# Attention with a top-32 mask, then a mixture of experts, on one core: another order for the scores, one VectorE shift, the reads of the value sums and the late tails of the transposes

## The chip, the cores and the metric

The kernel runs on one core of one Trainium2 chip. The metric is the device time of one execution in microseconds (us). The core has five engines with queues of their own: TensorE (PE, with its weight loads as PEld), VectorE (DVE), ScalarE (ACT), GpSimd (POOL) and SyncE (SP, which issues most transfers). Each engine takes its instructions strictly in the order in which they are written in the kernel; between engines only waits on semaphores keep order.

## The reference, cut to what matters

```python
# attention: q, k, v are (2, 8, 576, 64)
scores = scale * np.matmul(q, k.transpose(0, 1, 3, 2))
kth = np.partition(scores, -32, axis=-1)[..., -32:-31]
scores = np.where(scores >= kth, scores, -1e9)
scores = scores - np.max(scores, axis=-1, keepdims=True)
attn = np.exp(scores)
attn = attn / (np.sum(attn, axis=-1, keepdims=True) + 1e-09)
x = np.matmul(attn, v)          # then reshaped to (1152, 512)
# mixture of 8 experts: each token goes to the expert of its largest logit
h = np.maximum(np.einsum('ecd,edf->ecf', disp, w1), 0.0)
y = np.einsum('ecf,efd->ecd', h, w2)
out[i] = gate_w[i] * y[expert_idx[i], pos[i]]
```

## The kernel before, in words

Attention is worked off in 36 units. A unit `u` is one block of 128 query rows (9 blocks) with one pair of heads (4 pairs); heads of a pair are `j` = 0 and 1, each row has 576 scores. The function `attention` runs a loop of 35 iterations; unit 35 and the leftovers follow by hand. In iteration `i` different steps of different units stand beside each other (a software pipeline), and the order of the calls in this loop is the order in every engine's queue:

- `scores(u)`: PE multiplies queries and keys into three PSUM banks, tile `s0` (two banks: all of head 0, and the first 64 columns of head 1) and tile `s1` (the other 512 columns of head 1). There is one copy of these tiles, so `scores(i+1)`, issued in iteration `i`, has to wait until everything that reads unit `i`'s scores is through.
- `heads(i)`: DVE takes the 8 largest of each 64-column segment (18 MAX8, L312), then the row maximum `mx` (L315), a masked copy (L316), and at the end the shift "max minus score" of 64 columns of head 1 into the tile `sm` (L318). These 64 columns lie in the second bank of `s0`.
- `shift(i)`: ACT shifts the remaining columns, 576 of head 0 out of `s0` and 512 of head 1 out of `s1` (two activations, L353).
- `merge(i)`: DVE looks for the pivot among the segments' maxima (MAX8 `ns` L329, MATCH_REPLACE8 L334, MAX8 L336 and L337); `bound` finishes it one iteration later.
- `sign(i-1)` and `turn(i-1)`: ACT counts, POOL multiplies, giving the tile `z`; `select(i-2)`: DVE takes two MAX8 over 576 columns of `z` (steps 1 and 2, L393), and two small steps to the threshold `nk` (L397).
- `penalty(i-3)`: ACT writes the tile `pen` (two activations, L406) from `nk`; `probs(i-3)`: PE transposes `sm` plus `pen` in 9 blocks (L425, L426), ACT takes the exponential (L427).
- `values(i-4)`: PE multiplies with the values (L447, L450) into the bank `pV`, in two halves (one per head); `normalise(i-5)` on DVE reads it (L461, L463, L466).
- `route(t, stage)`: the router of a finished block of tokens, in stages over some eight iterations: stage 0 transposes on PE, stage 0.5 copies them with ACT (`copies()`, L519), stage 1 multiplies with the gate (L522), stages 2 to 2.2 pick the expert, 3 to 5.5 find the slot and scatter the row.

Short DVE steps (`small`: `bound`, `select` 0, `normalise`, router steps, the picks of experts in `early` and `late`) are taken one after another between the 18 MAX8 of `heads`: `fill()` issues the next one, 16 times per unit; what is left follows after `heads`.

Iterations 3 to 30 hold the 9 transposed blocks in one PSUM tile `p3` (`whole` is true). In iterations 31 to 34 they go in three steps of 4, 4 and 1 blocks; the last one, the tail, then uses columns 384 to 511 of the bank `pV` and is issued after `scores(i+1)`. From iteration 31 on PE also works on the first expert in quarters (`quarter_h`, L654; ACT takes the result at L701).

The order on PE in an iteration is: transposes of `probs(i-3)`, `values(i-4)`, router stages 1 and 3, `scores(i+1)`, (late tail), router stage 0. After attention the experts follow, bound to the routed tokens.

Of the kernel before, what the change touches and what calls it, by code (L numbers as in the profile page):

```python
# [19 lines left out]
FT = mybir.dt.float32  # L20
# [5 lines left out]
OP = mybir.AluOpType  # L26
BIG = float(2.0 ** 90)
LOW = -3.0e38
# [7 lines left out]
def kernel(  # L36
# [11 lines left out]
    nc = tc.nc  # L48
    B, H, S, D = q.shape
# [13 lines left out]
    P = {}  # L63
# [14 lines left out]
    def att(*a, **k):  # L78
        return P["att", 0].tile(*a, **k)
# [31 lines left out]
    TAIL = S - 512  # L111
# [173 lines left out]
    PS, VAL, SM, Z, NK, PEN, PT = {}, {}, {}, {}, {}, {}, {}  # L285
# [18 lines left out]
    def heads(u, fill):  # L304
        un = UN[u % 2]
        nn = att([128, 2, SEG, 5], FT, name="nn")
        SM[u] = att([128, 2, S], FT, name="sm", tag="sm", bufs=4)
        mx = att([128, 4, 2], FT, name="mx4", bufs=3)
        for j in range(2):
            for i in range(SEG):  # L310
                o = int(i < FOUR)
                nc.vector.max(out=un[:, j, i, o:o + 8], in_=segment(u, j, i))  # L312
                if i < SEG - 1:
                    fill()
        nc.vector.tensor_reduce(out=mx[:, 0], in_=un[:, :, :, 0:2], axis=mybir.AxisListType.XY, op=OP.max)  # L315
        nc.vector.scalar_tensor_tensor(nn, un[:, :, :, 0:5], -1.0, keep[:, None].to_broadcast([128, 2, SEG, 5]),  # L316
                                       op0=OP.mult, op1=OP.min)
        nc.vector.tensor_scalar(SM[u][:, 1, :TAIL], PS[u][0][:, S:S + TAIL], -1.0, mx[:, 0, 1:2], op0=OP.mult, op1=OP.add)  # L318
        VAL[u] = [mx, un, nn.rearrange("p j s c -> p j (s c)")]

    def merge(u, fill):
        mx, un, nn = VAL[u]
        wk = att([128, 2, 5 * SEG], FT, name="wk")
        na = att([128, 2, 8], FT, name="na")
        tm = att([128, 2, 8], FT, name="tm")
        ns = att([128, 2, 8], FT, name="ns")
        vb = VB[u % 2]
        for j in range(2):
            nc.vector.max(out=ns[:, j], in_=nn[:, j])  # L329
        if u == NU - 1:  # L330
            fill()
        fill()
        for j in range(2):
            nc.vector.match_replace(out=wk[:, j], in_to_replace=ns[:, j], in_values=nn[:, j], imm_value=LOW)  # L334
        for j in range(2):
            nc.vector.max(out=vb[:, j], in_=un[:, j, :, 5:])  # L336
            nc.vector.max(out=na[:, j], in_=wk[:, j])  # L337
        fill()
        VAL[u] = [mx, na, vb, tm]
# [11 lines left out]
    def shift(u):  # L351
        for j, (o, i) in enumerate(((SM[u][:, 0], PS[u][0][:, :S]), (SM[u][:, 1, TAIL:], PS[u][1]))):
            nc.scalar.activation(o, i, AF.Identity, bias=VAL[u][0][:, 0, j:j + 1], scale=-1.0)  # L353

    SEL, SG = {}, {}

# [53 lines left out]
    def probs(u, *steps):  # L410
        sm = SM[u].rearrange("p j s -> p (j s)")
        pen = PEN[u].rearrange("p j s -> p (j s)")
        whole = ("p3", 0) in P
        if 0 in steps:
            PT[u] = att([128, 9, 128], FT, name="pT", tag="pT")
        for step in (0,) if whole else steps:
            if whole:
                bs, pt = range(9), P["p3", 0].tile([128, 9, 128], FT, name="p3", bufs=1)
            elif step < 2:
                bs, pt = range(5 * step, 5 * step + 4), bank4()  # L420
            else:
                bs, pt = (4,), pv[:, None, 384:512]
            for i, c in enumerate(bs):
                cs = slice(128 * c, 128 * c + 128)
                nc.tensor.matmul(pt[:, i], sm[:, cs], ident, start=True, stop=False, is_transpose=True)  # L425
                nc.tensor.matmul(pt[:, i], pen[:, cs], identB, start=False, stop=True)  # L426
            nc.scalar.activation(PT[u][:, bs[0]:bs[-1] + 1], pt, AF.Exp, scale=-scale)  # L427

    PV, XR = {}, {}
    pv = psum.tile([128, 512], FT, name="pV", bufs=1)  # L430
# [42 lines left out]
    TAIL_P = []  # L473
# [448 lines left out]
    NU = NT * HP  # L922
# [120 lines left out]
    def attention(side, early, late, mid, act, pool, end):  # L1043
        nc.vector.memset(OHS, 0.0)
        def run(fs):
            for f, *a in fs:
                f(*a)

        for i in range(NU - 1):
            if i == FUSED[0]:  # L1050
                swap_psum("pt", "p3")
            if i == FUSED[1]:
                swap_psum("p3", "pt")
            whole = ("p3", 0) in P

            def routes(stages):
                res = []
                for st in stages:
                    t, r = divmod(i - 6 - int(st), HP)
                    if r == HP - 1 and 0 <= t < NT:  # L1060
                        res.append((route, t, st, nc.vector if t == NT - 1 else nc.gpsimd))
                return res

            def copies():
                t, r = divmod(i - 7, HP)
                return [(route, t, 0.5, None)] if r == HP - 1 and t >= 0 else []

            def at(lag, f, *a):
                return [(f, i - lag) + a] if 0 <= i - lag < NU else []

            small = []

            def fill():
                if small:
                    run([small.pop(0)])

            small += at(1, bound, 0) + at(1, bound, 1) + at(1, bound, 2) + at(2, select, 0) + early.get(i, [])
            small += at(5, normalise, 0) + at(5, normalise, 1) + at(5, normalise, 2) + routes((2, 2.1, 2.2, 4, 5, 5.5)) + late.get(i, [])
            run((copies() + at(3, penalty) if whole else at(3, penalty) + copies()) + at(0, heads, fill))
            while small:  # L1080
                fill()
            run((at(1, sign_turn, act.get(i, []), pool.get(i, [])) if i > 1 else []) + side.get(i, []))
            last = i == NU - 2
            exps, tails = (at(3, probs, 0), []) if whole else (at(3, probs, 0, 1), at(3, probs, 2))
            run(exps + at(0, shift) if last else at(0, shift) + exps)
            run(at(4, values) + routes((1, 1.5, 3)) + at(-1, scores) + tails + routes((0, 3.5)))
            run(mid.get(i, []) + at(2, select, 1) + at(2, select, 2))
            small += at(2, select, 3) + at(2, select, 4)
            if last:
                small += [(route, NT - 3, 2, nc.gpsimd)]  # L1090
            run(at(0, merge, fill))
            while small:
                fill()
            run(end.get(i, []))
            if last:
                values(i - 3)


        L, T = NU - 1, NT - 1
        small = []  # L1100
# [31 lines left out]
        drop()  # L1132
        run(side.get(L, []))
        shift(L)
        penalty(L - 2, (1,))
        merge(L, fill)
        swap_psum("sc", "bk")
# [98 lines left out]
    pt = [bank1().bitcast(HF) for _ in range(2)]  # L1236
# [149 lines left out]
```

## Time and profile before

| | us |
|---|---|
| median of 3 runs (lowest to highest) | 385.41 (385.14 to 385.71) |
| time of the profiled execution | 387.18 |
| its span, first to last instruction | 385.4 |
| busy in the span: PE / PEld | 327.9 / 266.8 |
| busy in the span: DVE / ACT / POOL | 320.5 / 277.9 / 240.0 |

The profiled execution is one of its own, so its time stands 1.8 us above the median; some 1.8 us of it lie around the span. Times of instructions below are us from the start of the span. In rows of the timeline the first number is the start, the second the duration, then engine, line, operation, the tiles as out<-in, their shape, and in brackets how long the engine sat idle before it and what ended that.

### The profile page before, as it was taken

The page shows a single profiled execution, that of the slowest core. Times are in us where ns is not written, and L with a number is a line of the kernel's source. Part 1 is how long each engine was busy: PE and PEld are TensorE (multiplying, and loading weights), DVE is VectorE, ACT ScalarE, POOL GpSimd, SP SyncE. Part 2 cuts the span into 40 slices and gives each one's busy share as a digit, 9 for nine tenths or more (in the row PEclk, how much of TensorE's full clock was granted, in tenths as well). Part 3 has the DMA queues.
Part 4 walks back from the last instruction along what each step waited for, and adds up shares of the span by engine and source line. Part 5 has one row for each costly group of instructions (what it writes and reads, how often), then busy time and mean ns, then how long its engine had stood idle before and what let it go on. Part 6 is the DMA issues. An engine that isn't in the chain of part 4 may idle for free. (4 is left out here: it accounts for less than half of the span.)

```text
span 385.4 us, 9927 instructions
## 1 busy us (share of the span) xinstructions
PE 327.9 (85%) x3383; PEld 266.8 (69%) x3383; DVE 320.5 (83%) x1708; ACT 277.9 (72%) x464; POOL 240.0 (62%) x280
## 2 busy tenths in 40 slices
PE   5676978797888887978898889898879999999991
PEld 3454857585766765756586678788834899997781
DVE  4888699999999999999999998857664778799940
ACT  5788688888887878888789587766256649586810
POOL 3975868588886697988988788964301101119521
PEclk9778699999999999999989899989999999999997
DMA  9629996937282920000211730730849999999400
GB/s 153 133 63 195 219 199 203 207 113 125 40 265 79 344 106 3 30 2 29 57 54 44 225 117 28 247 111 29 295 144 268 204 351 401 340 300 400 83 23 23
DMA packets 69922, 60.25 MB, mean 156 GB/s; under 512 B 52069, under 2 KB 52069, under 8 KB 69863
## 3 DMA queue, kind: packets, MB, share of 16 engines
q1 hardware_dynamic: 67719, 54.79, 52.0%
q0 software_dynamic: 1616, 4.73, 3.4%
q8 instruction: 28, 0.46, 0.5%
q14 instruction: 31, 0.25, 0.2%
q10 hardware_dynamic: 528, 0.02, 0.1%
HBM read 40.66 MB, written 12.09 MB: 137 GB/s over the span
## 5 line engine op out<-in xcount | busy, mean ns | idle before, releaser
L312 DVE MAX8 un<-s 128x8 f32<-128x64 f32 x648 | 107.1, 216 | 12.8 <-PE s L294 12.8
L369 POOL TENSOR_TENSOR z<-sm,sg 128x576 f32<-128x576 f32 x71 | 89.5, 1280 | 24.0 <-ACT sg L362 22.0
L674 POOL DMA_INDIRECT out_dram<-y,xp x12 | 25.5, 2122 | 79.3 <-DVE y L850 39.1
L450 PE MATMUL pV<-vm,pT 128*128 128x65 f32 (+1 forms) x640 | 69.9, 267 | 0.0
L450 PEld LDWEIGHTS pV<-vm,pT 128*128 128x128 f32 (+1 forms) x640 | 68.9, 186 | 0.0
L353 ACT ACTIVATE sm<-s,mx 128x576 f32<-128x576 f32 x72 | 47.4, 710 | 25.4 <-DVE sm L318 23.6
L615 DVE TENSOR_TENSOR ws<-wr,ws 128x1024 bf16<-128x1024 f32 x52 | 60.7, 1215 | 2.6 <-ACT ws L609 2.5
L425 PE MATMUL p<-ident,sm 128*128 128x128 f32 x252 | 52.3, 293 | 9.8 <-ACT pT L427 5.6
L362 ACT ACTIVATE sg<-sm,mx 128x576 bf16<-128x576 f32 x72 | 55.0, 766 | 3.1 <-DVE mx L348 2.6
L426 PE MATMUL p<-identB,pen 128*128 128x128 bf16 x252 | 47.2, 227 | 9.8 <-ACT pen L406 9.8
L294 PE MATMUL s<-qk 128*128 128x512 f16 (+3 forms) x320 | 45.7, 301 | 8.7 <-ACT sm L353 8.6
L406 ACT ACTIVATE pen<-sm,nk 128x576 bf16<-128x576 f32 x71 | 51.2, 769 | 2.4 <-DVE nk L397 0.9
L425 PEld LDWEIGHTS p<-ident,sm 128*128 128x128 f32 x252 | 37.0, 147 | 22.0 <-ACT pT L427 12.3
L609 ACT ACTIVATE ws<-wr 128x2048 f16<-128x2048 f32 (+1 forms) x26 | 47.6, 1842 | 5.3 <-issue 4.4
L393 DVE MAX8 z<-z 128x8 f32<-128x576 f32 x72 | 50.8, 745 | 0.0
L654 PEld LDWEIGHTS <-ws 128*128 128x128 f16 (+1 forms) x768 | 48.8, 98 | 1.0 <-issue 0.4
L426 PEld LDWEIGHTS <-pen 128*128 128x128 bf16 x324 | 34.3, 108 | 16.1 <-ACT pen L406 14.3
L294 PEld LDWEIGHTS <-qk 128*128 128x128 f16 (+1 forms) x320 | 20.5, 108 | 20.1 <-issue 12.4
L427 ACT ACTIVATE pT<-p 128x1152 f32<-128x1152 f32 x28 | 31.6, 1130 | 0.0
L615 POOL TENSOR_TENSOR ws<-wr,ws 128x1024 bf16<-128x1024 f32 x12 | 25.6, 2132 | 0.0
L447 PE MATMUL pV<-vt,pT 128*128 128x130 f32 (+1 forms) x80 | 18.4, 313 | 4.9 <-DVE pD L960 1.8
L835 PEld LDWEIGHTS <-ws 128*128 128x128 f16 (+1 forms) x288 | 21.3, 98 | 0.0
(273 smaller groups left out, 640.9 us busy)
## 6 DMA issues: line engine op xcount, KB each, us to landing
wr<-in_moe_w_dram SPq DMA_DIRECT2D x32, 1024.0 KB, 6.2
xbuf<-zero SPq DMA_DIRECT2D x6, 771.0 KB, 5.0
qnat<-in_q_dram SPq DMA_DIRECT2D x16, 144.0 KB, 3.8
knat<-in_k_dram SPq DMA_DIRECT2D x16, 144.0 KB, 4.1
out_dram<-zero SPq DMA_DIRECT2D x3, 768.0 KB, 4.7
vm<-in_v_dram SPq DMA_DIRECT2D x16, 128.0 KB, 3.0
qk<-qk SPq DMA_DIRECT2D x14, 144.0 KB, 2.4
vt<-in_v_dram SPq DMA_DIRECT2D x4, 64.0 KB, 3.1
```

The costliest lines, as they stand in the source:

```text
L294: nc.tensor.matmul(PS[u][a][row:row + n, o:o + w], QK[b][2 * i][:, h, s:s + n], QK[b][1][:, h, c:c + w], start=(i == 0), stop=(i == 1))
L312: nc.vector.max(out=un[:, j, i, o:o + 8], in_=segment(u, j, i))
L362: nc.scalar.activation(SG[u][j], SM[u][:, j], AF.Sign, bias=VAL[u][0][:, 2, j:j + 1], scale=-(1.0 - 2.0 ** -20), accum_out=CNT[:, c:c + 1])
L369: engs[j].tensor_tensor(out=Z[u][:, j], in0=SM[u][:, j], in1=SG[u][j], op=OP.mult)
L393: nc.vector.max(out=z8[:, step - 1], in_=Z[u][:, step - 1])
L406: eng.activation(o, x, AF.Relu, bias=n)
L425: nc.tensor.matmul(pt[:, i], sm[:, cs], ident, start=True, stop=False, is_transpose=True)
L426: nc.tensor.matmul(pt[:, i], pen[:, cs], identB, start=False, stop=True)
L450: nc.tensor.matmul(PV[t][row:row + n, h0 + half], PT[u][:, 5 * half + c, row:row + n], VM[b][:, c, p, half], start=False, stop=(half == 1 ...
L609: nc.scalar.activation(w[:, 0, s], r[:, s], AF.Copy)
L615: eng.tensor_tensor(out=w[:, 1].bitcast(BF)[:, s], in0=r[:, s], in1=w[:, 0, s], op=OP.subtract)
L654: nc.tensor.matmul(o, a(i), c(i), start=(i == 0 and m == 0), stop=(i == k - 1 and m == 2))
```

## The change

Four things are moved, nothing is computed differently:

1. `values(i-4)` is cut: half 0 stands before `scores(i+1)`, half 1 and all router stages behind it.
2. The 64-column shift leaves `heads` and becomes `shift_rest`. On DVE the order after `heads` is now: `select` step 1 (first MAX8 over `z`), the two `ns` maxima of `merge` (half 0), `shift_rest`, `select` step 2 (second MAX8 over `z`), then the rest of `merge` (half 1). In the order of the kernel the 64-column shift now stands behind ACT's `shift`.
3. In the list `small`, `early` and `late` come ahead of `normalise`, filled up with empty entries to at least four, so that `normalise` and the router's reads come four fills later.
4. The tail of the transposes gets a bank of its own (`ex`) in iterations 31 to 34 and is issued with the other two steps; in all iterations `penalty` stands ahead of `copies()` on ACT.

```diff
-        nc.vector.tensor_scalar(SM[u][:, 1, :TAIL], PS[u][0][:, S:S + TAIL], -1.0, mx[:, 0, 1:2], op0=OP.mult, op1=OP.add)
...
+    def shift_rest(u):
+        nc.vector.tensor_scalar(SM[u][:, 1, :TAIL], PS[u][0][:, S:S + TAIL], -1.0, VAL[u][0][:, 0, 1:2],
+                                op0=OP.mult, op1=OP.add)
...
-    def merge(u, fill):
-        mx, un, nn = VAL[u]
+    def merge(u, fill, half=None):
+        mx, un, nn = VAL[u][:3]
+        if half != 1:
+            ns = att([128, 2, 8], FT, name="ns")
+            for j in range(2):
+                nc.vector.max(out=ns[:, j], in_=nn[:, j])
+            VAL[u] = [mx, un, nn, ns]
+            if half == 0:
+                return
+            fill()
+        ns = VAL[u][3]
...
-                bs, pt = (4,), pv[:, None, 384:512]
+                bs, pt = (4,), (pv if TAIL_P else P["pt", 0].tile([128, 512], FT, name="ex", bufs=1))[:, None, 384:512]
...
-            small += at(1, bound, 0) + at(1, bound, 1) + at(1, bound, 2) + at(2, select, 0) + early.get(i, [])
-            small += at(5, normalise, 0) + at(5, normalise, 1) + at(5, normalise, 2) + routes((2, 2.1, 2.2, 4, 5, 5.5)) + late.get(i, [])
-            run((copies() + at(3, penalty) if whole else at(3, penalty) + copies()) + at(0, heads, fill))
+            small += at(1, bound, 0) + at(1, bound, 1) + at(1, bound, 2) + at(2, select, 0)
+            small += [(lambda: None,)] * (4 - len(early.get(i, []) + late.get(i, [])))
+            small += early.get(i, []) + late.get(i, [])
+            small += at(5, normalise, 0) + at(5, normalise, 1) + at(5, normalise, 2) + routes((2, 2.1, 2.2, 4, 5, 5.5))
+            run(at(3, penalty) + copies() + at(0, heads, fill))
...
-            exps, tails = (at(3, probs, 0), []) if whole else (at(3, probs, 0, 1), at(3, probs, 2))
+            exps = at(3, probs, 0, 1, 2)
             run(exps + at(0, shift) if last else at(0, shift) + exps)
-            run(at(4, values) + routes((1, 1.5, 3)) + at(-1, scores) + tails + routes((0, 3.5)))
-            run(mid.get(i, []) + at(2, select, 1) + at(2, select, 2))
+            picks = at(2, select, 1) + at(0, merge, None, 0) + at(0, shift_rest) + at(2, select, 2)
+            run(at(4, values, 0) + picks + at(-1, scores) + at(4, values, 1) + routes((1, 1.5, 3)) + routes((0, 3.5)))
+            run(mid.get(i, []))
...
-            run(at(0, merge, fill))
+            run(at(0, merge, fill, 1))
...
         shift(L)
+        shift_rest(L)
```

## Rows read from the trace of the kernel before

**Rows 1.** Busy time by stretch: PE, PEld, DVE, ACT, POOL, then clock, DMA share, GB/s.

```profile
50.00:210.00 160.00, 134.03 (x1278) 107.93 (x1279) 154.55 (x1070) 136.01 (x242) 130.71 (x145) 0.99 0.41 113
...
297.00:350.00 53.00, 53.00 (x714) 51.12 (x713) 43.95 (x49) 37.25 (x42) 8.69 (x6) 1.00 1.09 326
```

**Rows 2.** Waits, whole span: who waited for whom, us in total, times, longest.

```profile
DVE un L312 <- PE s L294: 12.8, 13, 2.9
...
ACT sm L353 <- DVE sm L318: 23.6, 25, 2.3
```

**Rows 3.** Waits of DVE from 50 to 210 us.

```profile
DVE un L312 <- PE s L294: 4.3, 6, 0.9
```

**Rows 4.** Waits of DVE from 210 to 240 us.

```profile
DVE un L312 <- PE s L294: 2.4, 3, 1.1
```

**Rows 5.** Timeline of DVE, end of unit 23's heads to unit 24's first MAX8.

```profile
161.82 0.19 DVE L315 TENSOR_REDUCE mx<-un 128x2 f32<-128x36 f32 x1
161.93 0.24 DVE L316 SCALAR_TENSOR_TENSOR nn<-un,pD 128x90 f32<-128x90 f32 x1
162.09 0.28 DVE L318 TENSOR_SCALAR sm<-s,mx 128x64 f32<-128x64 f32 x1
162.28 1.41 DVE L393 MAX8 z<-z 128x8 f32<-128x576 f32 x2
163.61 0.29 DVE L329 MAX8 ns<-nn 128x8 f32<-128x45 f32 x2
...
164.76 0.22 DVE L312 MAX8 un<-s 128x8 f32<-128x64 f32 x1
```

**Rows 6.** Timeline of ACT and PE in the same stretch.

```profile
162.46 1.32 ACT L353 ACTIVATE sm<-s,mx 128x576 f32<-128x576 f32 x2 [1.33 <-DVE sm L318]
...
163.25 1.17 PE L294 MATMUL s<-qk 128*128 128x512 f16 x8 [0.72 <-ACT sm L353]
```

**Rows 7.** Timeline of iteration 22, one with copies() and router stage 1.

```profile
152.25 0.60 ACT L519 ACTIVATE xT<-p 128x512 f32<-128x512 f32 x1 [0.75 <-PE p L513]
152.75 1.43 ACT L406 ACTIVATE pen<-sm,nk 128x576 bf16<-128x576 f32 x2
153.57 0.23 PE L426 MATMUL p<-identB,pen 128*128 128x128 bf16 x1 [0.33 <-ACT pen L406]
157.02 1.06 PE L522 MATMUL pV<-wg,xT 128*128 128x8 f32 x8
157.93 1.14 PE L294 MATMUL s<-qk 128*128 128x512 f16 x8
158.68 0.23 DVE L312 MAX8 un<-s 128x8 f32<-128x64 f32 x1 [0.71 <-PE s L294]
```

**Rows 8.** Timeline of iteration 2, ACT and DVE.

```profile
28.37 1.31 ACT L353 ACTIVATE sm<-s,mx 128x576 f32<-128x576 f32 x2
...
29.91 0.23 DVE L312 MAX8 un<-s 128x8 f32<-128x64 f32 x1 [1.16 <-PE s L294]
```

**Rows 9.** Timeline of iteration 4, PE and DVE.

```profile
39.85 3.52 PE L450 MATMUL pV<-vm,pT 128*128 128x65 f32 x16
...
44.47 0.23 DVE L312 MAX8 un<-s 128x8 f32<-128x64 f32 x1 [2.87 <-PE s L294]
```

**Rows 10.** Waits of ACT from 210 to 250 us.

```profile
ACT pT L427 <- PE pV L426: 6.1, 4, 2.1
```

**Rows 11.** Timeline of DVE and PE in unit 35, around the last tail in pV.

```profile
247.14 0.16 DVE L461 TENSOR_SCALAR rs<-pV 128x4 f32<-128x4 f32 x1 [1.35 <-ACT pT L427]
...
248.12 0.46 PE L447 MATMUL pV<-vt,pT 128*128 128x130 f32 x2 [1.64 <-DVE xr L466]
```

**Rows 12.** Timeline of PE in iteration 24, the values.

```profile
167.43 1.90 PE L450 MATMUL pV<-vm,pT 128*128 128x65 f32 x16
```

**Rows 13.** Busy time by stretch around one drop of the clock; columns as in Rows 1.

```profile
188.65:192.06 3.41, 1.94 (x13) 0.89 (x12) 3.41 (x25) 3.15 (x5) 3.41 (x4) 1.00 0.41 79
192.06:195.47 3.41, 3.39 (x21) 2.90 (x21) 3.38 (x22) 2.51 (x6) 2.91 (x3) 0.51 0.56 231
```

More of the change, by code (lines that the diff above doesn't have):

```diff
@@ L325, in merge @@
         tm = att([128, 2, 8], FT, name="tm")
-        ns = att([128, 2, 8], FT, name="ns")
         vb = VB[u % 2]
         for j in range(2):
-            nc.vector.max(out=ns[:, j], in_=nn[:, j])
-        if u == NU - 1:
-            fill()
+            nc.vector.match_replace(out=wk[:, j], in_to_replace=ns[:, j], in_values=nn[:, j], imm_value=LOW)
         fill()
-        for j in range(2):
-            nc.vector.match_replace(out=wk[:, j], in_to_replace=ns[:, j], in_values=nn[:, j], imm_value=LOW)
         for j in range(2):
```

## The prediction

> **What bounds the kernel now.** I read the busy time by stretch first. From 50 to 210 us, where units 6 to 30 run, DVE is busy 154.55 of 160 us, PE 134, ACT 136, POOL 131 [rows 1]: DVE sets the pace, and only what makes DVE idle or adds work to it counts there. The views of waits then say what makes it idle: 12.8 us in 13 units, each time the first MAX8 of a unit waiting for PE's scores [rows 2]; 4.3 us of it in six units between 50 and 210 us [rows 3], 2.4 us in three units from 210 to 240 us [rows 4], 2.87 us in unit 5 [rows 9]; the other three waits, of about 1.1 us each, are units 1 to 3, the last of which is in [rows 8]. From 297 to 350 us PE is busy for all of 53.00 us [rows 1]: the experts run as one block behind attention, so time saved in attention should arrive at the end undiminished.
>
> Next the timeline of one normal unit. After `mx` starts at 161.82, DVE does L316, the 64-column shift L318, two MAX8 over z, two `ns`, and 2.94 us after `mx` the next unit's MAX8 can begin [rows 5]. ACT's shift begins at 162.46, 0.09 us after L318 ends (162.37), although `mx` is ready at 162.01 [rows 5, 6]. That is so 25 times, 23.6 us in all [rows 2]. The two touch different columns, but of one PSUM bank: the program keeps their order. PE's scores start at 163.25, 0.79 us after ACT's shift started and well before both of its activations end (162.46 + 1.32) [rows 6]; so what waits for a tile waits for the one activation that it needs.
>
> Last a late unit, number 23. In iteration 22 the copy L519 waits 0.75 us for PE and holds `pen` back to 152.75; PE then does transposes, all values, the gate product L522 at 157.02, and only then the scores at 157.93; DVE, free at 157.97, starts at 158.68 [rows 7]. The six waits stand four units apart: it is this router pattern that repeats.
>
> **The change, part by part.**
>
> *Scores ahead of half the values and of the router.* In iteration 22, L522 alone holds the scores from 157.02 to 157.93, 0.91 us [rows 7], and half of the values, about 0.95 us of 1.90 [rows 12], goes behind them too. PE is thus ready some 1.9 us earlier, against a wait of 0.71 us. What is late next is the end of the shifts, below, at 1.49 us after `mx`; MAX8 can start some 0.75 us after the scores (158.68 - 157.93), so 2.24 us after `mx`, while DVE is busy for 2.94. No wait is left: I take all 4.3 us (bounds 0 and 4.3). What is queued behind the moved half: router products and the next transposes. `normalise`, which reads the sums, comes four fills later, that is behind four more MAX8 of at most 0.22 us each [rows 5], 0.9 us in all, which covers the 0.95; for DVE they are the same instructions, so this costs nothing. Uncovered, it would be a wait of up to 0.95 us in every second unit.
>
> In unit 5 PE is at half speed: the 16 value products take 3.52 us [rows 9], against 1.90 [rows 12]. Half of them is 1.76: I take 1.8 of the 2.87 us (bounds 0; 2.87 if the slow spell moves away).
>
> *`penalty` ahead of `copies`.* ACT sat idle from 151.50 to 152.25 and copied until `pen` could start at 152.75 [rows 7]. In the new order `pen` starts up to 1.25 us earlier and the copy follows at about 153.0 if PE's transposes are there, to end at about 153.5; PE's first masked block started at 153.57 before [rows 7]. So PE gains nothing and ACT is done with its signs about 0.6 us earlier, early enough to start its shift on time. Cost 0; uncovered, the copy holds PE by its 0.60 us in six units (3.6), which the lead of 1.9 us hides.
>
> *The 64-column shift between the maxima.* It is the same instruction: DVE's sum stays. ACT may now start 0.09 us after L315, at `mx` + 0.28 instead of + 0.64. But the order in the bank turns round: the DVE shift now waits for ACT's first activation, done for its waiter by 0.28 + 0.79 = 1.07 us after `mx`. Its own place in DVE's queue is 0.27 (L316 done) + 0.67 (one MAX8 over z) + 0.22 (two `ns`) = 1.16 [rows 5]. So there is 0.09 us to spare, and the scores may start at 1.16 + 0.28 + 0.05 = 1.49 instead of 163.25 - 161.82 = 1.43: no gain in itself, and harmless, since DVE is busy until 2.94. Queued behind it on DVE: the second MAX8 over z, the threshold, the pivot and the next unit. Where ACT is late, DVE now stands. Iteration 2 is such a place: ACT's shift starts only at 28.37 [rows 8]. DVE's shift can follow at 29.16, and then 0.19 + 0.67 and the 0.93 us that remain of the 2.94 (164.76 - 162.09 less 0.19, 1.33 and 0.22) end at 30.95, where unit 3's MAX8 began at 29.91 [rows 5, 8]: a loss of 1.0 us (bounds 0, if no order were kept, and 1.3).
>
> The Trainium skill (PSUM — Partial Sum Buffer, "PSUM bank collisions raise a hardware error") asks that two engines be kept apart by bank, reads against reads too, not by address. It speaks against this step: by it the DVE shift must wait as worked out above. The trace agrees (0.09 us after L318, 25 times); if only addresses counted, the sum would be 1.0 us better.
>
> *Late tails in their own bank.* ACT waits 6.1 us in four iterations for the tails behind the scores [rows 10]. With them ahead, `pen` and all that follows on ACT come about 1.2 to 2 us earlier, which these iterations need to be on time for the new DVE wait. The three waits for scores there, 2.4 us [rows 4], go as the others do; but the relu of the expert's quarter now comes behind half of the values, so ACT can still be late in two units by some 0.25 us: 2.4 - 0.5 = 1.9 (bounds 0 and 2.4). In unit 35 `normalise` waits 1.35 us for the tail's exponential, and PE's next values wait 1.64 for `normalise` [rows 11]; the tail of that unit no longer sits in pV. Half the values and the router stand behind the scores there, and give some back: 0.8 (bounds 0 and 1.64).
>
> *TensorE's pauses.* Before, PE's idle time in a unit lay in several pieces; now it gathers ahead of the scores. With values of 0.95 us done by about 168.4 and the scores not before `mx` (168.10) + 1.49, one pause is 1.2 us. A stretch in which PE was busy 1.94 of 3.41 us at clock 1.00 was followed by one at 0.51, the level of 1.2 GHz [rows 13]. Such a spell does 1.7 us less work in 3.4 us; PE's idle share of 26 in 160 us [rows 1] covers 0.55 of that, so a spell costs up to 1.15 us, less where DVE has a lead. I take 0.5 in all (bounds 0 and 9.2: a spell in each of eight groups of four units).
>
> **The sum.** 4.3 + 1.8 + 1.9 + 0.8 - 1.0 - 0.5 = 7.3 us. Against its own execution (387.18, of which 385.4 span) that gives 379.9; the median of the runs is 1.77 lower, 385.41, and from there 378.1.
>
> **Rivals.**
>
> *DVE waits in every unit (slower).* If the 64-column shift has to wait for both activations of ACT, it can start at 0.28 + 1.32 = 1.60 instead of 1.16: 0.44 us in some 33 units, 14.5, against 7.3 gained: 392.6. It decides the sign from 0.22 us per unit on, that is, if ACT's first shift were ready later than 1.38 after `mx`. For it: only 0.09 us to spare. Against it: PE's masked block began at 153.57 while the second `pen` ran on to 154.18 [rows 7], and the scores at 163.25 [rows 6]; single activations are waited for. Chance 0.13.
>
> *The clock falls at the gathered pauses.* Four spells at 1.15 more: 382.7. For it: [rows 13]. Against it: the scores then come later only into DVE's lead of 0.7 us. Chance 0.14. The Trainium skill (TensorE: Matmul & The Clock Gate, "Part 1: The HAM clock gate") calls the throttled state the default, which activity releases; by that rule gathered pauses are what to fear. The rows agree on the two levels.
>
> *The gain doesn't arrive.* Either PE's lead is eaten by its own queue (transposes behind the moved work), or the experts' transfers don't move with attention; the DMA share there is 1.09 [rows 1]. For it: that share; against it: PE has no gap there. About 385. Chance 0.07.
>
> **The numbers.** My forecast, 378.1, has 0.66. With all bounds good it is 4.3 + 2.87 + 2.4 + 1.64 - 1.0 = 10.2, so 375.2, less 0.3 for the runs' scatter; its bad end is about 381.5. To leave out no more than 2 in 10 the range takes in the clock's case: 374.9 to 384.0; no change and slower stay outside. A change under 0.2% (0.8 us) can't be told from none. Faster 0.79 (the first and most of the clock's case), same 0.07, slower 0.14.
>
> **What would show it.** Right: DVE's waits for scores between 50 and 240 us under 1 us; ACT's shift 0.3 us after `mx`; the DVE shift in iteration 2 waiting some 2 us for ACT; no tail waits on ACT; the experts' block starting about 7 us earlier. Wrong: L318's successor idle on ACT in most units, more stretches at half clock after 50 us, or a later block of the same distance from attention's end.

## The result, and the profile after

The changed kernel takes 380.0 us (median of four runs, 377.82 to 381.15) against 385.27 (385.05 to 385.71): ratio 0.9855, 95% interval 0.9809 to 0.9901. That is 5.3 us faster, inside the forecast range, 1.9 us above the forecast of 378.1. Its profiled execution took 379.64 us, 7.5 less than the profiled one of before. Ratios and their intervals, here and below, leave out the runs that took more than 1.5% longer than the fastest of their kernel.

Where the time came from is seen first in the chain that ended last. Of the kernel before, the first piece of the experts' block on PE and the last scatter (start, duration, what):

```profile
296.87 3.64 PE pT L758 x32
...
378.76 0.98 POOL out_dram L674
```

The same two pieces of the changed kernel:

```profile
288.05 3.64 PE pT L765 x32
...
370.01 0.98 POOL out_dram L681
```

The experts' block starts 8.82 us earlier and its length is the same (81.89 and 81.96 us from the first of these pieces to the last): all the difference is made before it, and all of it arrives at the last scatter. Behind that scatter the span goes on for 5.66 us before (385.4 less 379.74) and for 6.81 us after (377.8 less 370.99); so the spans differ by 7.6 only.

Busy time of the changed kernel in the stretch of [rows 1], same columns:

```profile
50.00:210.00 160.00, 132.59 (x1299) 110.41 (x1298) 157.66 (x1089) 138.12 (x245) 134.33 (x150) 1.00 0.44 116
```

DVE is now busy for 157.66 of 160 us instead of 154.55. Its waits from 50 to 210 us, all that are listed:

```profile
DVE pD L990 <- PE pV L962: 0.3, 1, 0.3
DVE pD L967 <- PE pV L962: 0.3, 1, 0.3
```

The six waits for scores of [rows 3] are gone. Waits of the whole span that are new or replace those of [rows 2] (L356 is ACT's shift, L359 the 64-column shift, L404 the threshold `nk`):

```profile
ACT pen L413 <- DVE nk L404: 20.5, 34, 1.9
...
PE s L294 <- DVE sm L359: 16.8, 25, 1.7
...
ACT sm L356 <- DVE mx L315: 9.0, 15, 2.0
...
DVE sm L359 <- ACT sm L356: 4.1, 5, 2.2
```

ACT now waits for the threshold, that is, it is early; PE waits for the 64-column shift before the scores, which costs nothing as long as DVE is busy meanwhile; and DVE's own new wait, which the slower rival expected in every unit, occurs five times. One normal unit on DVE, from the last three MAX8 before `mx` to the next unit's first MAX8, to be laid beside [rows 5]:

```profile
156.94 0.48 DVE L312 MAX8 un<-s 128x8 f32<-128x64 f32 x3
157.45 0.19 DVE L315 TENSOR_REDUCE mx<-un 128x2 f32<-128x36 f32 x1
157.56 0.24 DVE L316 SCALAR_TENSOR_TENSOR nn<-un,pD 128x90 f32<-128x90 f32 x1
157.71 0.76 DVE L400 MAX8 z<-z 128x8 f32<-128x576 f32 x1
158.38 0.30 DVE L325 MAX8 ns<-nn 128x8 f32<-128x45 f32 x2
158.60 0.27 DVE L359 TENSOR_SCALAR sm<-s,mx 128x64 f32<-128x64 f32 x1
158.78 0.75 DVE L400 MAX8 z<-z 128x8 f32<-128x576 f32 x1
...
159.79 0.17 DVE L402 SCALAR_TENSOR_TENSOR ds<-pD,z 128x16 f32<-128x16 f32 x1
159.99 0.21 DVE L339 MAX8 pD<-un 128x8 f32<-128x36 f32 x1
...
160.52 0.22 DVE L312 MAX8 un<-s 128x8 f32<-128x64 f32 x1
```

The 64-column shift stands 1.15 us after `mx` without a wait (forecast 1.16). ACT's shifts, the counterpart of [rows 6], begin 0.29 us after `mx` (forecast 0.28):

```profile
157.74 1.32 ACT L356 ACTIVATE sm<-s,mx 128x576 f32<-128x576 f32 x2 [0.29 <-PE p L433]
```

But from `mx` to the next MAX8 it is 3.07 us, where it was 2.94 [rows 5]: the same instructions cost 0.13 us more. The whole of it lies at `ds` (step 3 of `select`): it begins at 159.79, and the next instruction, which writes the bank that `ds` reads, only 0.20 us later. Before, `ds` stood ahead of the two MATCH_REPLACE8 and took 0.07 us:

```profile
163.82 0.15 DVE L395 SCALAR_TENSOR_TENSOR ds<-pD,z 128x16 f32<-128x16 f32 x1
163.89 0.08 DVE L334 MATCH_VALUE_LOAD wk<-ns,nn 128x8 f32 x1
```

Its new place is a fifth move, which the list of the change does not name and whose lines its diff leaves out: in the rewritten `merge` the `fill()` that issues `ds` comes only behind them.

```diff
+            nc.vector.match_replace(out=wk[:, j], in_to_replace=ns[:, j], in_values=nn[:, j], imm_value=LOW)
         fill()
-        for j in range(2):
-            nc.vector.match_replace(out=wk[:, j], in_to_replace=ns[:, j], in_values=nn[:, j], imm_value=LOW)
```

A whole unit became only 0.06 to 0.07 us longer (5.80 to 5.86 us between two `mx`, in every second unit 6.28 to 6.35), because half of the loss is won back in the next unit's MAX8, where DVE compares ACT's counts (`select` 0, L390 and now L397). Before, with the semaphore instruction that DVE has to take ahead of it:

```profile
165.38 0.22 DVE L312 MAX8 un<-s 128x8 f32<-128x64 f32 x1
165.57 0.18 DVE L390 TENSOR_TENSOR pD<-pD,CNT 128x16 f32<-128x16 f32 x1
165.66 0.22 DVE L312 MAX8 un<-s 128x8 f32<-128x64 f32 x1
...
L390 DVEq EVENT_SEMAPHORE  x33: 21/21/21, 23.6 to 233.6; - x33
```

After:

```profile
161.14 0.23 DVE L312 MAX8 un<-s 128x8 f32<-128x64 f32 x1
161.29 0.17 DVE L397 TENSOR_TENSOR pD<-pD,CNT 128x16 f32<-128x16 f32 x1
161.36 0.88 DVE L312 MAX8 un<-s 128x8 f32<-128x64 f32 x6
...
L397 DVEq EVENT_SEMAPHORE  x1: 21/21/21, 23.2 to 23.2; - x1
```

The semaphore instruction is gone in all units but one, and from the MAX8 ahead of the comparison to the one behind it DVE takes 0.21 us (median of the 24 units) instead of 0.28. It is there 33 or 34 times in the kernels whose 64-column shift stands in `heads`. The likely reason is that the moved shift waits for a later step of ACT, which covers the counts; that reason is not shown.

Iteration 2, the counterpart of [rows 8], on DVE:

```profile
28.75 0.28 DVE L359 TENSOR_SCALAR sm<-s,mx 128x64 f32<-128x64 f32 x1 [2.18 <-ACT sm L356]
```

### The profile page after: what moved, and what is told of

Its sections match the earlier page's. It is cut to its first block, busy times and chain, and to the rows that moved or that the text cites. A ratio compares the mean times of both kernels' runs of the same rounds, so it can differ in the third digit from the quotient of the medians.

```text
span 377.8 us, 9896 instructions
## 1 busy us (share of the span) xinstructions
PE 318.9 (84%) x3383; PEld 264.7 (70%) x3383; DVE 321.4 (85%) x1708; ACT 278.5 (74%) x464; POOL 240.0 (64%) x280
## 5 line engine op out<-in xcount | busy, mean ns | idle before, releaser
L457 PEld LDWEIGHTS pV<-vm,pT 128*128 128x128 f32 (+1 forms) x640 | 72.3, 183 | 6.9 <-issue 3.6
L681 POOL DMA_INDIRECT out_dram<-y,xp x12 | 24.4, 2032 | 79.8 <-DVE y L857 40.2
L457 PE MATMUL pV<-vm,pT 128*128 128x65 f32 (+1 forms) x640 | 73.2, 262 | 0.0
L622 DVE TENSOR_TENSOR ws<-wr,ws 128x1024 bf16<-128x1024 f32 x52 | 61.9, 1238 | 3.3 <-ACT ws L616 2.9
L294 PE MATMUL s<-qk 128*128 128x512 f16 (+3 forms) x320 | 44.0, 297 | 16.8 <-DVE sm L359 16.8
L432 PE MATMUL p<-ident,sm 128*128 128x128 f32 x252 | 50.0, 286 | 7.3 <-ACT xT L526 7.2
L400 DVE MAX8 z<-z 128x8 f32<-128x576 f32 x72 | 54.0, 752 | 1.3 <-POOL z L376 1.3
L356 ACT ACTIVATE sm<-s,mx 128x576 f32<-128x576 f32 x72 | 47.5, 711 | 9.7 <-DVE mx L315 9.0
L433 PE MATMUL p<-identB,pen 128*128 128x128 bf16 x252 | 46.0, 223 | 7.7 <-ACT pen L413 7.7
L661 PEld LDWEIGHTS <-ws 128*128 128x128 f16 (+1 forms) x768 | 49.0, 98 | 0.9 <-issue 0.4
L563 POOL DMA_INDIRECT xbuf<-xs,ru x9 | 10.5, 1166 | 17.2 <-DVE un L312 8.1
```

The costliest lines, as they stand in the source:

```text
L294: nc.tensor.matmul(PS[u][a][row:row + n, o:o + w], QK[b][2 * i][:, h, s:s + n], QK[b][1][:, h, c:c + w], start=(i == 0), stop=(i == 1))
L400: nc.vector.max(out=z8[:, step - 1], in_=Z[u][:, step - 1])
L457: nc.tensor.matmul(PV[t][row:row + n, h0 + half], PT[u][:, 5 * half + c, row:row + n], VM[b][:, c, p, half], start=False, stop=(half == 1 ...
L622: eng.tensor_tensor(out=w[:, 1].bitcast(BF)[:, s], in0=r[:, s], in1=w[:, 0, s], op=OP.subtract)
L661: nc.tensor.matmul(o, a(i), c(i), start=(i == 0 and m == 0), stop=(i == k - 1 and m == 2))
```

## The experiments

The times of one kernel scatter from run to run (the changed kernel had 377.8 to 381.2, the unaltered kernel before 381.7 to 389.2 over all sets), so each verdict rests on medians together with places in the trace: the starts of the experts' block, and of `mx` in units 6 and 30, whose difference is called the middle. Before: block at 296.87, middle 153.60. After: 288.05 and 150.48.

**The changed kernel once more.** No edit.

> The changed kernel once more, unaltered, to see how far its time scatters beside the others on one chip. Expected 380.0 us, 377.8 to 381.2 as in its four runs. If the forecast's 7.3 us fell short (5.3 measured) because the profiled execution of the kernel before was a slow one of its kind, the difference of the medians stays near 5.3; if the four runs were unlucky, it comes nearer to 7.

Measured: 378.81 us (377.76 to 380.17, six runs), beside 385.0 of the kernel before; ratio 0.9862 (0.9826 to 0.9897). Block at 287.50, middle 150.33. So the gain is 5.3 to 6.2 us, and not 7.3. The forecast's terms came from one execution that took 387.18 us, 1.9 above its kernel's median.

**The order on PE undone.**

```diff
-run(at(4, values, 0) + picks + at(-1, scores) + at(4, values, 1) + routes((1, 1.5, 3)) + routes((0, 3.5)))
+run(at(4, values) + picks + routes((1, 1.5, 3)) + at(-1, scores) + routes((0, 3.5)))
```

> The changed kernel with both halves of the values and the router's products back ahead of the scores on PE; all else as changed. Theory 1 (the order on PE is the gain): the six waits of DVE for scores between 50 and 210 us come back, 4.3 us, and part of the 2.4 us after that: 384 to 387. Theory 2 (the gain is ACT's, through penalty and tails): at most 381.5 and no waits for scores.

Measured: 389.62 us beside 386.84 of the kernel before, ratio 1.0151 (1.0066 to 1.0237): slower than the kernel before, by more than either theory said. Block at 298.50, middle 156.57. DVE's waits from 50 to 210 us:

```profile
DVE un L312 <- PE s L294: 5.9, 5, 2.4
```

The order on PE carries the gain, and the other edits without it do harm. Four of the five waits are 0.82 to 0.94 us, about as in [rows 3]; the fifth, of 2.4 us in unit 15, follows a drop of the clock. PE had stood idle for 1.83 us in one piece, and from 101.4 us on the granted clock was 0.50, the level of 1.2 GHz:

```profile
100.48 0.33 PE L432 MATMUL p<-ident,sm 128*128 128x128 f32 x1 [1.83 <-ACT xT L526]
...
101.40:104.80 3.40, 3.40 (x20) 3.15 (x19) 3.33 (x20) 2.89 (x5) 2.67 (x3) 0.50 0.48 86
```

So the forecast's rival of the gathered pauses is seen here, where the values stand ahead of the scores, and not in the changed kernel between 50 and 210 us.

**Only the order on PE and the later reads**, on the kernel before.

```diff
-run(at(4, values) + routes((1, 1.5, 3)) + at(-1, scores) + tails + routes((0, 3.5)))
+run(at(4, values, 0) + at(-1, scores) + at(4, values, 1) + routes((1, 1.5, 3)) + tails + routes((0, 3.5)))
```

> The kernel before with only two of the four edits: scores between the halves of the values with the router behind, and the reads four fills later. Theory 1: DVE's waits for scores between 50 and 210 us vanish (4.3), unit 5 gains 0 to 2.9, ds and the 64-column shift keep their cheap places: 378.5 to 381. Theory 2: without penalty ahead of copies, ACT is late by some 1.6 us in every fourth unit and the waits for scores stay in part: 382 to 385.

Measured: 382.43 us (ten runs), ratio 0.991 (0.9858 to 0.9963). Block at 289.64, middle 149.66, the shortest of the kernels up to here: no wait for scores from 50 to 210 us, and units of 5.80 and 6.29 us. What it lacks is at the end, where DVE's waits from 240 to 262 us still hold the tails in pV:

```profile
DVE r L547 <- ACT pT L427: 4.8, 1, 4.8
...
DVE rs L461 <- ACT pT L427: 1.1, 1, 1.1
```

Its median lies in theory 2's range, its mechanism is theory 1's: that holds for the middle. The late copies, which theory 2 feared, did not bring the waits for scores back: DVE's shift stands ahead of ACT's here, so a late ACT holds only PE, which has the time.

**Copies ahead of penalty again.**

```diff
-run(at(3, penalty) + copies() + at(0, heads, fill))
+run((copies() + at(3, penalty) if whole else at(3, penalty) + copies()) + at(0, heads, fill))
```

> The changed kernel with copies() ahead of penalty again, as before. Theory 1: the router's transposes now stand behind the second half of the values and are ready about 4.3 us after mx; ACT waits for them, penalty and the signs move 1.4 us back, ACT's next shift starts about 1.6 us after mx, and DVE's 64-column shift waits for it by some 1.2 us in six units: 7 us, 387. Theory 2: the lead covers it: 380.0.

Measured: 381.49 us (ten runs), ratio 0.9903 (0.9857 to 0.9948); block at 291.21, middle 153.38, 2.9 us longer. ACT's wait for the router's transposes, 50 to 210 us:

```profile
ACT xT L526 <- PE p L520: 8.2, 6, 1.5
```

and DVE's wait for ACT in the same six units:

```profile
DVE sm L359 <- ACT sm L356: 2.8, 6, 0.6
```

The mechanism is as theory 1 had it, its size is 0.5 us per unit instead of 1.2. So this edit is needed, but only because the 64-column shift waits for ACT: in the experiment before, with the copies ahead but the shift in `heads`, the waits stayed away.

**Reads four fills earlier again.**

```diff
-small += [(lambda: None,)] * (4 - len(early.get(i, []) + late.get(i, [])))
-small += early.get(i, []) + late.get(i, [])
-small += at(5, normalise, 0) + at(5, normalise, 1) + at(5, normalise, 2) + routes((2, 2.1, 2.2, 4, 5, 5.5))
+small += early.get(i, [])
+small += at(5, normalise, 0) + at(5, normalise, 1) + at(5, normalise, 2) + routes((2, 2.1, 2.2, 4, 5, 5.5)) + late.get(i, [])
```

> The changed kernel with normalise and the router's reads four fills earlier, as before. Theory 1: the second half of the values ends about 3.65 us after mx, and normalise would read at about 4.0, so it still fits; only the router's read of the gate product (ready at 4.7) would wait 0.3 us in six units: 380 to 382. Theory 2: the later reads carry the change: without them DVE waits about 0.4 us or more in every second unit, 386 or more.

Measured: 379.71 us, ratio 0.987 (0.9789 to 0.9951); middle 150.79, so in normal units the later reads are worth nothing, as theory 1 said. Block at 290.94 in its profiled execution (381.39 us, the slowest of four): once, between 210 and 240 us, a router read waits 3.0 us, where the same read waits 1.2 us in the changed kernel:

```profile
DVE r L540 <- PE pV L529: 3.0, 1, 3.0
```

The medians show no loss from it.

**Tails in pV again**, issued behind the scores in iterations 31 to 34.

```diff
-bs, pt = (4,), (pv if TAIL_P else P["pt", 0].tile([128, 512], FT, name="ex", bufs=1))[:, None, 384:512]
+bs, pt = (4,), pv[:, None, 384:512]
...
-exps = at(3, probs, 0, 1, 2)
+exps, tails = (at(3, probs, 0), []) if whole else (at(3, probs, 0, 1), at(3, probs, 2))
...
-    routes((1, 1.5, 3)) + routes((0, 3.5)))
+    routes((1, 1.5, 3)) + tails + routes((0, 3.5)))
```

> The changed kernel with the tails back in pV, issued behind the scores, in iterations 31 to 34. Theory 1: ACT waits for the tails again (6.1 us before), its shifts of units 32 to 34 come 1 to 2 us late and DVE's 64-column shift waits for them; 2 to 4 us slower than the changed kernel: 382 to 384. Theory 2 (the tails are hidden behind PE's work there): 380.

Measured: 382.11 us, ratio 0.9935 (0.9862 to 1.0008); block at 294.21, middle unchanged at 150.48. ACT's wait, from 205 to 250 us, beside [rows 10]:

```profile
ACT pT L434 <- PE pV L433: 8.4, 4, 3.1
```

In this execution the block starts 6.2 us later, and in the medians 2 to 3 us are lost: the tails' bank is the second part of the gain. Its size stays open. The four runs fall into pairs: 380.2 and 380.4 us at a mean granted clock of 0.98, 0.2 to 1.6 us above the changed kernel's medians, and 383.82 and 384.88 at 0.955. The profiled one is of the second pair, and part of its 6.2 us is the clock. Its busy time from 240 to 262 us, columns as in [rows 1]:

```profile
240.00:262.00 22.00, 19.43 (x185) 17.98 (x183) 14.16 (x70) 14.27 (x32) 17.72 (x24) 0.84 0.49 162
```

The same stretch of the changed kernel:

```profile
240.00:262.00 22.00, 20.07 (x229) 18.96 (x228) 16.11 (x65) 15.29 (x33) 18.16 (x23) 1.00 0.41 154
```

**ACT's two shifts in the other order.** The activation over `s1` first, so that DVE's shift has to wait for both.

```diff
-for j, (o, i) in enumerate(((SM[u][:, 0], PS[u][0][:, :S]), (SM[u][:, 1, TAIL:], PS[u][1]))):
+for j, (o, i) in ((1, (SM[u][:, 1, TAIL:], PS[u][1])), (0, (SM[u][:, 0], PS[u][0][:, :S]))):
```

> The changed kernel with ACT's two shift activations in the other order (512 columns of s1 first), so that the 64-column shift on DVE has to wait for both. Theory of the forecast's rival: DVE waits 0.44 to 0.48 us in each unit, some 15 us: 394 to 396. Other theory (the spare time on DVE hides it): 380 to 383.

Measured, one run: 394.1 us; block at 303.46, middle 162.27. DVE's waits from 50 to 210 us:

```profile
DVE sm L359 <- ACT sm L356: 9.4, 24, 0.4
```

0.39 us in each of 24 units, and the middle is 11.8 us longer: the forecast's slower rival, brought about by this edit, came out at its price (14.5 us were worked out; this run is 14.1 above the changed kernel's median). DVE waits for an activation that reads other columns of the same bank. That agrees with what the forecast cited from the Trainium skill (PSUM — Partial Sum Buffer, "PSUM bank collisions raise a hardware error"), two reads being kept apart by bank and not by address; whether this program goes by bank or by tile no run here separates.

**The 64-column shift back in heads**, `ns` still between the maxima.

```diff
-picks = at(2, select, 1) + at(0, merge, None, 0) + at(0, shift_rest) + at(2, select, 2)
+picks = at(2, select, 1) + at(0, merge, None, 0) + at(2, select, 2)      # shift_rest(u) at the end of heads
```

> The changed kernel with the 64-column shift back at the end of heads, ahead of ACT's shift; all else as changed. Theory 1: the shift's new place gains nothing by itself and costs DVE's wait of 2.18 us in iteration 2, some 1 us: 379.0, and scores start 1.43 us after mx instead of 1.47. Theory 2: ACT's start at mx + 0.29 instead of + 0.64 is what keeps ACT on time in the units of 5.8 us: then ACT falls behind by up to 0.35 us in each unit and the time is 381 to 390.

Measured: 379.48 us, ratio 0.9884 (0.9843 to 0.9924); block at 288.34. The median doesn't tell the two places apart. The trace does: iteration 2 is 1.1 us shorter, as theory 1 says, but the middle is 152.09, with units of 5.93 and 6.40, 1.6 us longer than in the changed kernel. The semaphore instruction ahead of the comparison is back (34 times), which theory 1 did not have: the new place does gain something in itself, 0.07 us per unit.

**`ds` ahead of the MATCH_REPLACE8**, on the changed kernel.

```diff
-        for j in range(2):
-            nc.vector.match_replace(...)
-        fill()
+        fill()
+        for j in range(2):
+            nc.vector.match_replace(...)
```

> The changed kernel with the small threshold step ds (L402) put back ahead of the two MATCH_REPLACE8, as it stood before. Theory 1: in the changed kernel ds reads the bank pD directly ahead of a MAX8 that writes pD, and takes 0.20 us of DVE's time instead of 0.07, so each unit is 0.07 us longer than before (5.86 and 6.35 instead of 5.80 and 6.28). Put back, 0.07 to 0.13 us in some 33 units: 2.3 to 4.3 us faster than the changed kernel, 375.7 to 377.7. Theory 2: the 0.07 us come from the 64-column shift between the two maxima over z; then nothing changes, 380.0.

Measured: 379.01 us, ratio 0.9876 (0.9838 to 0.9915); middle 150.54, units of 5.87 and 6.35: no change, theory 1 falls in this form. Its timeline says why:

```profile
158.35 0.75 DVE L400 MAX8 z<-z 128x8 f32<-128x576 f32 x1
159.13 0.17 DVE L402 SCALAR_TENSOR_TENSOR ds<-pD,z 128x16 f32<-128x16 f32 x1
159.22 0.08 DVE L337 MATCH_VALUE_LOAD wk<-ns,nn 128x8 f32 x1
```

`ds` now begins 0.78 us after the maximum that it needs, where the next instruction otherwise follows after 0.67 (158.78 to 159.45 would be its place in the changed kernel). The 0.11 us have only moved: from the instruction behind `ds` to `ds` itself. In the kernel before, the `ns` pair stood between the second maximum and `ds`.

**The same `ds` ahead, and iteration 2's 64-column shift ahead of ACT's.**

```diff
-            picks = at(2, select, 1) + at(0, merge, None, 0) + at(0, shift_rest) + at(2, select, 2)
+            picks = at(2, select, 1) + at(0, merge, None, 0) + (at(0, shift_rest) if i != 2 else []) + at(2, select, 2)
...
+            if i == 2:
+                shift_rest(i)
             run(exps + at(0, shift) if last else at(0, shift) + exps)
```

> The changed kernel with ds ahead of MATCH_REPLACE8 (as in e1_threshold_first), and in iteration 2 alone the 64-column shift ahead of ACT's shift, so that DVE need not wait there. Theory 1: 2.3 to 4.3 us of the first and 1.0 of the second add up: 374.7 to 376.7. Theory 2 (the 0.07 us are the shift's own; what iteration 2 saves is lost again in the wait for scores that stood there before, 1.16 us): 379 to 380.

Measured: 379.2 us, ratio 0.9858 (0.9808 to 0.9907). Block at 286.20. In iteration 2 `mx` of unit 3 comes 6.39 us after that of unit 2, instead of 8.15 in the changed kernel and 7.51 in the experiment before; the middle stays at 150.54; in medians nothing of it can be told from the scatter.

**Another instruction between.** The changed kernel with iteration 2 as above, and

```diff
-            nc.vector.max(out=vb[:, j], in_=un[:, j, :, 5:])
             nc.vector.max(out=na[:, j], in_=wk[:, j])
+            nc.vector.max(out=vb[:, j], in_=un[:, j, :, 5:])
```

> The changed kernel with two small edits: in iteration 2 alone the 64-column shift ahead of ACT's shift (as in e9_both), and the MAX8 into na (L340) ahead of the one into pD (L339), so that ds and the instruction that waits for the same bank are one instruction apart. Theory 1 (an instruction right behind the one that it needs costs DVE about 0.13 us more; the ns pair used to stand between): units shrink from 5.86 and 6.35 to about 5.76 and 6.25, units 6 to 30 from 150.4 to about 148, the experts' block begins near 283.7, the median is 375 to 377. Theory 2 (the split of the z maxima costs 0.07 in any order): units stay at 5.86 and 6.35, only iteration 2 gains: block at 286.2, median 378 to 379.

Measured: 375.67 us (373.34 to 378.23), ratio 0.9768 (0.971 to 0.9825): the best of all, some 3 us below the changed kernel. Units of 5.76 and 6.25, middle 148.08; block at 285.78, 2 us later than expected: the first units ran slower in this execution than in the one before (`mx` of unit 6 at 52.01 instead of 49.58; from 35 to 42 us the granted clock was 0.55). Its timeline:

```profile
158.44 0.17 DVE L402 SCALAR_TENSOR_TENSOR ds<-pD,z 128x16 f32<-128x16 f32 x1
158.52 0.20 DVE L339 MAX8 na<-wk 128x8 f32<-128x45 f32 x1
158.64 0.21 DVE L340 MAX8 pD<-un 128x8 f32<-128x36 f32 x1
```

`ds` takes 0.08 us of DVE's time instead of 0.20. This is the theory of the instruction right behind the one that it has to wait for, in the form that holds.

**DVE's old order**, all else as changed: `shift_rest` in heads, both maxima over z, then `merge` in one piece.

```diff
-picks = at(2, select, 1) + at(0, merge, None, 0) + at(0, shift_rest) + at(2, select, 2)
+picks = at(2, select, 1) + at(2, select, 2)                             # shift_rest(u) at the end of heads
...
-run(at(0, merge, fill, 1))
+run(at(0, merge, fill))
```

> The changed kernel with DVE's old order: 64-column shift at the end of heads, both maxima over z behind it, then merge in one piece; PE's order, the later reads, penalty first and the tails' own bank stay. Theory 1: units go back to 5.80 and 6.28 or less, no wait in iteration 2, the block begins at about 285 to 286, median 377 to 378.5, that is, edit 2 of the change is worth nothing or less. Theory 2 (the shift between the maxima carries part of the gain): 380 or more.

Measured: 379.11 us (376.64 to 382.0), ratio 0.986 (0.9801 to 0.992); units of 5.81 and 6.29, middle 149.41, block at 286.80. In the trace 0.7 to 1.3 us better than the changed kernel, in the medians the same. So the second edit as it was made is worth nothing or slightly less. Four kernels of this section separate its two effects; units (short, long) and middle in us:

| | `ds` right ahead of an instruction that waits for it | another instruction between |
|---|---|---|
| 64-column shift in `heads` | 5.93, 6.40; 152.09 | 5.81, 6.29; 149.41 |
| 64-column shift between the maxima | 5.86, 6.35; 150.48 (the changed kernel) | 5.76, 6.25; 148.08 |

The new place gains 1.3 to 1.6 us in the middle in either column, the neighbour of `ds` costs 2.4 to 2.7 in either row.

## Why the prediction was right, by its own steps

*DVE is the bound, and it waits for PE's scores.* Right: with the waits gone its busy time in the stretch went from 154.55 [rows 1] to 157.66 us, and undoing the order on PE cost more than the whole gain (389.62 us, beside 386.84 of the kernel before). A slip of reading: five of the six waits stand four units apart (units 11 to 27), the sixth, of 0.43 us, is in unit 29.

*4.3 us from the six waits.* The waits went entirely, but the middle became only 3.1 us shorter (153.60 to 150.48). The step that was mis-sized is "It is the same instruction: DVE's sum stays". The moves left `ds` directly ahead of an instruction that has to wait for it: 0.13 us per unit there, of which 0.07 were won back by the semaphore instruction that fell away, 5.86 for 5.80. By the distances of `mx`, the seven units of the middle that had waited before (six for scores, one for ACT) became shorter by 4.2 us together, and the other 17 longer by 0.07 each, 1.1 us in all. The wait for ACT, before, from 50 to 210 us:

```profile
DVE pD L390 <- ACT pen L406: 0.3, 1, 0.3
```

Swapping two instructions took 0.10 us off each unit, more than the 0.07.

*1.8 us in unit 5.* The period of unit 5 fell from 8.76 to 5.86 us, 2.9: the upper bound, because PE was not at half speed there in this execution. From 35.0 to 45.2 us the granted clock was 0.50 before and 1.00 after. With PE's new order the period was 5.80 to 5.94 us in ten of the profiled executions and 6.82 in the one with the swapped pair (375.67 us), where the slow spell stood there again. Of the kernel before one execution alone was profiled, so whether the change or chance moved the spell stays open.

*The shift between the maxima: no gain in itself, a loss of 1.0 in iteration 2.* The loss is right in place and size: 0.09 us to spare sufficed, the shift stood at 1.15 us, and DVE waited 2.18 us in iteration 2, which made that unit 1.1 us longer (7.05 to 8.15). "No gain in itself" is not right: the semaphore instruction that falls away is worth 1.3 to 1.6 us in the middle, and the new neighbour of `ds` costs more than that.

*Penalty ahead of copies at no cost.* Right, and it is needed: without it 2.8 us of waits come back.

*1.9 us in units 31 to 34 and 0.8 at the end.* From unit 30's `mx` to unit 34's it was 0.9 us less (29.80 to 28.88); from unit 34's `mx` to the experts' block 2.75 less (59.86 to 57.11). The two terms together were 2.7, and came to 3.7, but the split between them was wrong. In units 31 to 34 the 2.4 us of waits for scores went, and DVE got new ones of 1.1 us instead, for PE's counts for the picks of experts (L962), for its values (L457) and for ACT's shift:

```profile
DVE pD L990 <- PE pV L962: 0.5, 2, 0.3
DVE sm L359 <- ACT sm L356: 0.3, 1, 0.3
DVE rs L468 <- PE pV L457: 0.3, 1, 0.3
```

Of the 1.5 us that did not come, this names 1.1; the rest stays open. At the end the clock helped: from 240 to 262 us it was 1.00 in place of 0.92 before, and how much of the 2.75 us is due to it and how much to the tails' bank no run separates.

```profile
240.00:262.00 22.00, 19.92 (x209) 18.17 (x208) 15.19 (x81) 14.17 (x31) 18.20 (x25) 0.92 0.48 158
```

*0.5 us for TensorE's clock.* Not paid between 50 and 210 us: the granted clock is 1.00 there (0.99 before, [rows 1]). PE was busy for 132.59 of the 160 us there, and its pauses ahead of the scores were of 0.7 to 0.9 us in normal units. They gathered and the clock stayed; that rival fell. From 210 to 240 us the clock was 0.94 in both kernels, and over the span it was higher after than before (0.970 against 0.953), so the term had the wrong sign in these two executions.

*The sum.* By the traces it is 8.8 us at the experts' block, above the 7.3 that were forecast; in the medians it is 5.3 to 6.2. Of this gap, 1.9 us are the profiled execution of before, which lay that far above its median (387.18 against 385.27); 1.15 us are the longer time behind the last scatter in the profiled execution of after. The rest, 0.4, is that the profiled execution of after lay below its median (379.64 against 380.0). Taking a gain from one execution's waits and subtracting it from the median was the weak part of the sum: waits that belong to that execution alone, such as unit 5's, may count in it in full. That the sum came so near is in part luck, since its errors cancel: the middle gave 1.2 us less than taken, unit 5, the end and the clock's term 2.6 more.

## What to carry to other kernels

Where one engine is the bound, look for what is queued ahead of the work that it waits for, and put that behind; half of a long step is often enough. When instructions are moved on the bound engine, the sum of their durations isn't the whole cost: see which two become neighbours, and keep something independent between a result and its reader. A wait that is turned round (the bound engine after a helper) is safe only by its spare time, here 0.09 us, and then every place where the helper is late has to be found. It can also make another wait superfluous, here 0.07 us per unit.

## What the runs showed of the hardware that was not expected

On DVE a short instruction directly behind one that it has to wait for starts 0.11 to 0.13 us later than an independent one would: 0.20 us against 0.07 for the one behind `ds`, 0.78 against 0.67 behind a MAX8 over 576 columns. Independent neighbours overlap: the next starts before the last has ended in every timeline above. Dependent ones start 0.03 us after that end, `mx` behind the last MAX8 of each unit too (156.94 + 0.48 = 157.42; 157.45). Whether the program's wait or the engine by itself holds them back, no run separates. The Trainium skill (VectorE: DVE Perf Modes, "The DRAIN you can't avoid") says of a chain of copies that a semaphore after each costs nothing extra, because the next one does not start until the pipe is empty, and that a next instruction which is not held starts earlier. The traces agree with the second (MAX8 of 0.22 us start 0.14 us apart). Against the first, losing that overlap costs 0.11 to 0.13 us here, and the measurement decides.

A semaphore instruction in DVE's own queue, of 21 ns by its row, cost 0.07 us per unit (0.28 against 0.21 us around the comparison with ACT's counts).

The scatter of a kernel's runs goes with TensorE's granted clock. Of the 41 runs of the kernel before that stand beside the experiments, the nine fastest (381.7 to 383.0 us) all had a mean clock of 0.970 or more, and the nine slowest (387.35 us and more) all 0.966 or less. Whether the clock makes those runs slow or is low because PE waits more in them, no run separates.

From the end of the last scatter's issue to the end of the span it took 5.66 us in one execution and 6.81 in another (5.2 to 6.8 over all 14 profiled ones): a difference of a fifth of the measured gain, in a part that no edit touched.
